# Rows of a weight tile padded from 642 to 648 columns, and one small copy moved from VectorE to ScalarE

## The chip, the cores and the metric

One core of one Trainium2 chip. The metric is the device time of one execution in microseconds (us).

## The reference

```python
x = A_x                                           # [1, 2048, 640] bf16
g = sigmoid((x * gate_w).sum(-1, keepdims=True))  # gate_w: 640
a = linear_attention(x, wqkv, w_phi, wo)          # 32 heads of 20, softmax feature maps
b = (silu(x @ w_gate) * (x @ w_up)) @ w_down      # 1728 wide
return g * a + (1 - g) * b
```

## The kernel before

The whole kernel is one static order of work. The change concerns its first microseconds and one tile, `wvg`, which holds the v part of `wqkv` and, as one more column, `gate_w`. A v projection of 128 tokens is ten matmuls into two PSUM banks: five rows `c` of the tile, each in two halves of 320 and 321 columns. The 321st column of the second half is the gate's sum.

```python
wvg = sb("wvg", [P, 5, D + 2], BF16)              # D = 640: a row is 642 columns, 1284 bytes

def v_pairs(t, pr):                               # ten matmuls for token tile t
    return [(bank(2 * pr + hb, 0, 320 + hb), xT[:, t, c, :],
             wvg[:, c, 320 * hb:640 + hb - 320 * (1 - hb)], c == 0, c == 4, False)
            for c in range(5) for hb in range(2)]

def xpose(t):                                     # "X": TensorE transposes an x tile, VectorE copies it out
    ...
def gcol():                                       # "G": gate_w, five rows of 128, becomes five columns
    pr = next_pair()
    o = bankbf(2 * pr, 8)[:, 0:5]
    transposes([(o, gwr[0:5, :])], 5)
    copy("dve", wvg[:, :, D:D + 1], o.unsqueeze(2))

def load_phi():                                   # "h": w_phi, issued by ScalarE once w3 has landed
    tr._wait("act", dict([wv_evs[3]]))
    dma("act", wph[:, :, :], ...)

LOADS = """x0 w0 x1 g w1 x2 w2 x3 w3 w4 f0 h k0 ..."""       # w0 to w4: rows of wvg; cut
ORDER = """H0 ... H12 X0 G X1 U0.0 U1.0 U0.1 X2 U1.1 U2.0 ...
... U0.4 U1.4 U2.4 V3 Y F0.1 M1 ...  K0 K1 ..."""            # cut
```

`H` are warm-up matmuls, `Ut.c` are the two matmuls of row `c` of v tile `t` (the first three tiles are done by rows, as their data land), `V` is a v tile in one go, `F` a piece of the feed-forward part, `M` premultiplies the k weights with blocks of w_phi that `Y` makes, `K` is a k projection. A helper puts a semaphore wait ahead of each instruction for what it reads and overwrites. Every engine does its instructions in this order.

The softmax here doesn't subtract the row's maximum and nothing guards it: scores larger than these inputs give would overflow.

## Time and profile before

| | kernel before |
|---|---|
| time, median of 3 | 288.74 us (288.39 to 288.85) |
| profiled span | 287.0 us |
| TensorE busy | 284.1 us, 99% |
| VectorE, ScalarE, GpSimd busy | 57%, 53%, 56% |

The prediction below shows the lines of the profile. A weight load (PEld) comes just ahead of its matmul (PE), and the idle time in brackets says what it waited for. And a matmul's end in the profile is modelled: a v matmul shows as 300 ns long, but the next one starts 136 ns later. What a matmul costs in a stream is the distance from its start to the next start.

### The profile page before, as it was taken

The numbers are of one execution on the slowest core, as the hardware profiler recorded it, in microseconds if no ns is written. First come the engines' busy times: TensorE is split into PE (matmuls) and PEld (weight loads), VectorE is DVE, ScalarE is ACT, GpSimd is POOL, SyncE is SP. The second block draws the span as 40 slices with busy tenths as digits, with TensorE's granted clock in tenths as the row PEclk, the third lists the DMA queues.
The fourth block names the chain that finished last, engine by engine and source line by source line (L and its number), as shares of the span: only waits on it lengthen the run. The fifth ranks groups of instructions, "written<-read, shape, count | busy, mean of one in ns | idle before, by whom it ended". The sixth has DMA issues, their size and how long they took to land.

```text
span 287.0 us, 4972 instructions
## 1 busy us (share of the span) xinstructions
PE 284.1 (99%) x1979; PEld 174.5 (61%) x1979; DVE 163.3 (57%) x243; ACT 152.4 (53%) x256; POOL 159.8 (56%) x125
## 2 busy tenths in 40 slices
PE   8999999999999999999999999999999999999997
PEld 6667777575644545557775556675554446666776
DVE  2337748576569978689991465970317899100000
ACT  0767778576775465683535753225676552234112
POOL 8286999879446789836543438350754558501000
PEclk9999999999999999999999999999999999999999
DMA  7977697000010598202383002061020006210101
GB/s 234 192 113 127 113 279 279 3 1 2 0 50 0 123 290 162 50 2 50 66 157 69 6 1 50 2 149 43 2 50 0 3 1 123 53 46 0 49 23 48
DMA packets 48944, 21.62 MB, mean 75 GB/s; under 512 B 39384, under 2 KB 48792, under 8 KB 48920
## 3 DMA queue, kind: packets, MB, share of 16 engines
q1 hardware_dynamic: 47400, 20.43, 31.5%
q10 hardware_dynamic: 1520, 0.87, 1.0%
q8 instruction: 16, 0.26, 0.4%
q14 instruction: 8, 0.07, 0.1%
HBM read 9.29 MB, written 2.62 MB: 42 GB/s over the span
## 4 chain that ended last, share of the span: by engine, by line
PE 99%; DVE 0%; issue 0%
PE ps L296 97%; PE ps L478 1%; PE ps L308 0%; DVE xT L320 0%; DVE osb L737 0%; DVE wvg L320 0%
## 5 line engine op out<-in xcount | busy, mean ns | idle before, releaser
L324 POOL TENSOR_TENSOR hT<-hT,us 128x512 bf16<-128x512 bf16 (+1 forms) x56 | 65.0, 1174 | 65.1 <-DVE hT L328 47.5
L328 DVE SCALAR_TENSOR_TENSOR hT<-hT,ps 128x512 bf16<-128x512 bf16 (+1 forms) x56 | 37.4, 683 | 66.8 <-ACT hT L314 53.0
L296 PE MATMUL ps<-xT,wg 128*128 128x512 bf16 x260 | 64.6, 379 | 0.0
L296 PE MATMUL ps<-xT,wu 128*128 128x512 bf16 x260 | 64.6, 379 | 0.0
L296 PE MATMUL ps<-wd,hT 128*128 128x320 bf16 (+2 forms) x462 | 63.9, 295 | 0.0
L324 POOL TENSOR_TENSOR ph<-eq,qc 128x1320 bf16<-128x1320 bf16 x16 | 42.4, 2647 | 25.6 <-DVE qc L638 20.8
L296 PEld LDWEIGHTS ps<-wd,hT 128*128 128x128 bf16 x462 | 44.5, 98 | 17.5 <-issue 0.2
L296 PE MATMUL ps<-wqk,xT 128*128 128x320 bf16 x320 | 47.7, 299 | 0.0
L314 ACT ACTIVATE hT<-ps 128x512 bf16<-128x512 f32 (+2 forms) x64 | 36.4, 569 | 16.8 <-PE ps L296 16.5
L296 PEld LDWEIGHTS ps<-xT,wu 128*128 128x128 bf16 x260 | 25.5, 98 | 30.6
L314 ACT ACTIVATE us<-ps 128x512 bf16<-128x512 f32 (+1 forms) x56 | 33.5, 598 | 18.5 <-PE ps L296 17.3
L314 ACT ACTIVATE osb<-ps,omg 128x640 bf16<-128x640 f32 (+2 forms) x17 | 12.9, 758 | 55.4 <-PE ps L296 55.4
L296 PEld LDWEIGHTS ps<-xT,wg 128*128 128x128 bf16 x260 | 25.1, 98 | 27.8 <-ACT osb L314 0.8
L324 POOL TENSOR_TENSOR ekr<-ekr,krec 128x1280 bf16<-128x1280 bf16 x16 | 37.4, 2358 | 5.8 <-DVE krec L338 5.8
L296 PEld LDWEIGHTS ps<-wqk,xT 128*128 128x128 bf16 x320 | 30.5, 98 | 13.1 <-issue 0.4
L314 ACT ACTIVATE eq<-ps 128x640 bf16<-128x640 f32 x32 | 22.4, 704 | 20.9 <-POOL ph L324 10.8
L335 DVE TENSOR_REDUCE ksum<-ekr 128x64 f32<-128x1280 bf16 x16 | 23.5, 1471 | 11.7 <-ACT ekr L314 11.7
L314 ACT ACTIVATE ekr<-ps 128x640 bf16<-128x640 f32 x32 | 22.3, 704 | 8.7 <-PE ps L296 8.2
L335 DVE TENSOR_REDUCE qz<-eq 128x64 f32<-128x1280 bf16 x16 | 23.6, 1478 | 2.6 <-ACT eq L314 2.6
L296 PE MATMUL ps<-wog,oT 128*128 128x320 bf16 (+2 forms) x165 | 24.7, 294 | 0.0
L296 PE MATMUL ps<-wvg,xT 128*128 128x320 bf16 (+1 forms) x160 | 24.1, 299 | 0.1
L335 DVE TENSOR_REDUCE qw<-ez 128x64 f32<-128x1280 bf16 x16 | 23.6, 1477 | 0.0
(73 smaller groups left out, 188.6 us busy)
## 6 DMA issues: line engine op xcount, KB each, us to landing
out_dram<-osb SPq DMA_DIRECT2D x15, 160.0 KB, 2.0
wd<-in_B_w_down_dram SPq DMA_DIRECT2D x1, 2080.0 KB, 9.2
wg<-in_B_w_gate_dram SPq DMA_DIRECT2D x1, 1040.0 KB, 10.0
wu<-in_B_w_up_dram SPq DMA_DIRECT2D x1, 1040.0 KB, 12.2
wg<-in_B_w_gate_dram SPq DMA_DIRECT2D x1, 800.0 KB, 6.1
wu<-in_B_w_up_dram SPq DMA_DIRECT2D x1, 800.0 KB, 7.7
wog<-in_A_wo_dram SPq DMA_DIRECT2D x2, 375.0 KB, 7.1
xs<-in_A_x_dram ACTq DMA_DIRECT2D x3, 160.0 KB, 4.2
```

Of the source, the lines that this page charges most:

```text
L296: last = pe.matmul(o, lhsT=l, rhs=r, start=st, stop=sp_, skip_group_check=sk)
L314: return run("act", lambda: act.activation(o, i, func, scale=scale), rd, [o])
L324: return run(e, lambda: eo.tensor_tensor(o, a, b, op), [a, b], [o])
L328: return run("dve", lambda: dve.scalar_tensor_tensor(out=o, in0=a, scalar=s, in1=b, op0=op0, op1=op1), rd, [o])
L335: return run("dve", lambda: dve.tensor_reduce(o, i, AX.X, ALU.add), [i], [o])
L478: last = pe.matmul(bank(2 * pr, 0, P), lhsT=c, rhs=c, start=True, stop=True)
```

## The change

The copy of the gate column goes to an engine that has nothing to do at that time. The w_phi load, at which ScalarE would otherwise stand first, goes behind it. The rows of the tile grow from 1284 to 1296 bytes.

```diff
-x0 w0 x1 g w1 x2 w2 x3 w3 w4 f0 h k0 k1 t4 ...
+x0 w0 x1 g w1 x2 w2 x3 w3 w4 f0 k0 k1 t4 ...
...
-H0 ... H12 X0 G X1 U0.0 U1.0 U0.1 X2 ...
+H0 ... H12 X0 G h X1 U0.0 U1.0 U0.1 X2 ...
...
-    wvg = sb("wvg", [P, 5, D + 2], BF16)
+    wvg = sb("wvg", [P, 5, D + 8], BF16)
...
-        copy("dve", wvg[:, :, D:D + 1], o.unsqueeze(2))
+        copy("act", wvg[:, :, D:D + 1], o.unsqueeze(2))
```

More of the change, by code (lines that the diff above doesn't have):

```diff
@@ L33 @@
 LOADS = """
-x0 w0 x1 g w1 x2 w2 x3 w3 w4 f0 h k0 k1 t4 k2 k3 k4 t5 t6 t7 t8 t9 t10 t11 t12 t13 t14 t15 q0 q1 q2 q3
+x0 w0 x1 g w1 x2 w2 x3 w3 w4 f0 k0 k1 t4 k2 k3 k4 t5 t6 t7 t8 t9 t10 t11 t12 t13 t14 t15 q0 q1 q2 q3
 q4 f1 f2
@@ L38 @@
 ORDER = """
-H0 H1 H2 H3 H4 H5 H6 H7 H8 H9 H10 H11 H12 X0 G X1 U0.0 U1.0 U0.1 X2 U1.1 U2.0 U0.2 U1.2 U2.1
+H0 H1 H2 H3 H4 H5 H6 H7 H8 H9 H10 H11 H12 X0 G h X1 U0.0 U1.0 U0.1 X2 U1.1 U2.0 U0.2 U1.2 U2.1
 X3 U2.2 U0.3 U1.3 U2.3 U0.4 U1.4 U2.4 V3 Y F0.1 M1 i3 M0 F0.0 M2 V4 M3 M4 K0 K1 I S0 V6 V5 S1 P0
```

## The prediction

> **What bounds the kernel now.** I read the page first (busy shares, then the chain that ended last), then the chain in order of time, then the timeline of the first 14 us, where everything that the change touches lies, and a table of stretches.
>
> From the page: the shares of busy time, and the chain that ended last by engine and by line.
>
> ```profile
> PE 284.1 (99%) x1979; PEld 174.5 (61%) x1979; DVE 163.3 (57%) x243; ACT 152.4 (53%) x256; POOL 159.8 (56%) x125
> ...
> PE 99%; DVE 0%; issue 0%
> PE ps L296 97%; PE ps L478 1%; PE ps L308 0%; DVE xT L320 0%; DVE osb L737 0%; DVE wvg L320 0%
> ```
>
> TensorE is the bound. No other engine is busy over 57%, and the chain is TensorE for 99% of the span. The last entry, the gate column's copy by VectorE, is the only thing of this change that stands on the chain. Its size is in the chain in order of time (start us, us, what):
>
> ```profile
> 3.77 0.72 PE ps L308 x5
> 4.50 0.02 issue
> 4.52 0.42 DVE xT L320
> 4.94 0.10 DVE wvg L320
> 5.04 0.05 issue
> 5.09 1.00 PE ps L296 x6
> 6.08 0.32 PE ps L308 x5
> ...
> 77.51 207.57 PE ps L296 x1275
> ```
>
> So VectorE copies the first x tile out of PSUM, copies the gate column behind it, and only then does TensorE start on the v projection, at 5.09. From there the chain is TensorE to the end. How much TensorE idles there is in the table of stretches (length, then busy us and count of each engine, granted clock, DMA share, GB/s):
>
> ```profile
> 3.70:5.10 1.40, 1.29 (x13) 0.84 (x13) 0.81 (x5) 0.00 (x0) 1.34 (x4) 1.00 1.00 325
> 5.10:6.00 0.90, 0.90 (x7) 0.54 (x8) 0.37 (x2) 0.00 (x0) 0.84 (x2) 1.00 1.04 358
> 100.00:285.00 185.00, 185.00 (x1169) 110.29 (x1166) 100.09 (x149) 86.96 (x139) 86.17 (x56) 1.00 0.26 59
> ```
>
> TensorE is idle for 1.40 - 1.29 = 0.11 us before the v projection, and not at all later as busy time counts it. Busy time hides short stalls, since the ends of matmuls are modelled, so I take the stalls from the weight loads in the timeline (start us, us, engine, what, idle time before it and what ended it):
>
> ```profile
> 4.52 0.42 DVE L320 COPY xT<-ps 128x512 bf16<-128x512 bf16 x1 [0.20 <-PE ps L308]
> ...
> 4.86 0.17 DVE L320 COPY wvg<-ps 128x5 bf16<-128x5 bf16 x1
> ...
> 5.08 0.66 PEld L296 LDWEIGHTS ps<-wvg,xT 128*128 128x128 bf16 x6 [0.28 <-DVE wvg L320]
> ...
> 5.95 0.28 PEld L308 LDWEIGHTS ps<-ident,xs 128*128 128x128 bf16 x5 [0.20 <-DMA xs<-in_A_x_dram]
> ...
> 7.30 0.40 ACTq L350 DMA_DIRECT2D wph<-in_A_w_phi_dram  x1
> ...
> 7.79 1.28 ACT L314 ACT_TABLE_LOAD   x1 [7.79 <-DMA wvg<-in_A_wqkv_dram]
> ...
> 9.46 0.71 ACT L314 ACTIVATE v1r<-ps 128x640 bf16<-128x640 f32 x1 [0.39 <-PE ps L296]
> ```
>
> Two stalls follow each other. Weight loads wait 0.28 us for the gate copy, run six matmuls, and then wait 0.20 us for the DMA of the third x tile (x2), whose completion the trace dates to 5.905. **The second one decides the case.** ScalarE in this time has nothing to do: its first instruction is the table load at 7.79, after the w_phi issue.
>
> **What the Trainium skill says.** "ScalarE: Activation LUTs", section "What ACT_TABLE_LOAD costs", gives about 1283 ns for the load, the same for every set, and 186 ns + 0.833 ns per element for an ACTIVATE with immediate scale and bias. The trace agrees on the first (1.28 us, 1283 ns). For 5 elements the second gives an estimate of 190 ns; the nearest in the trace, the 128x1 copy to svec, takes 165 to 224 ns. "SBUF — State Buffer", section "Operand start alignment", asks only that an operand start at a multiple of its element size, and says that this is about legality and that nothing was timed. "DMA: Bandwidth & Descriptors", section "How a descriptor splits into AXI transactions", has a descriptor pay extra beats when it doesn't start on 256 bytes; rows of 1296 bytes don't start there any more than rows of 1284. The trace shows no cost of the odd start: the 1280-byte packets of its DMA records take on average 55.1 ns for w3 and w4, which start 3 and 4 rows of 1284 bytes into the tile, and 55.0 ns for x1, whose rows start on 32 bytes.
>
> **The change part by part.**
>
> Padding: 642 to 648 columns, so each of the five rows starts 12 bytes further on, and the tile grows by 60 bytes. Tiles in this layout start on multiples of 32 bytes, so what follows moves by 64. No load gets larger: each still writes 1280 bytes a row. By the packets above the DMA gains nothing. Nor do the matmuls: those that read wvg take a mean of 299 ns, as do those of 320 columns that read wqk, whose rows are 1280 bytes. Worth: 0.
>
> VectorE loses one copy of 171 ns. It starts at 4.86 because the 0.42 us xT copy was ahead of it, not because its input was late: TensorE's gate transpose starts at 4.41 and ends at 4.60 (0.18 us). The next xT copy can start some 0.07 us earlier (4.93 to 4.86).
>
> ScalarE gets that copy. Its table load moves too, since it comes just before the first ACTIVATE. ScalarE's last issue ahead of it starts at 2.69 and takes 0.45 us, so the load would run from about 3.24 to 4.52 (in the kernel before it starts 0.09 us after the issue ahead of it). That is 0.08 us before the transpose ends. The copy would start at about 4.63 (0.04 us after its matmul, as the v1r copy at 9.465 after a matmul that ends at 9.429) and end at 4.63 + 0.19 = 4.82, against 5.03 now.
>
> So the first v matmul may start at 4.82 + 0.05 = about 4.88 instead of 5.09: **0.2 us gained at that place**, of which at most 0.11 us is idle time in the busy rows.
>
> What becomes of it: the six matmuls (U0.0, U1.0, U0.1) then end their issue 0.2 us earlier, and the transposes of x2 come next in TensorE's order. They can't start before x2 lands at 5.905. They start at 5.95 as before, and the stall of 0.20 us becomes about 0.4 us. From there everything stands as it did. Sum: -0.2 us at the first stall, +0.2 us at the second, **0.0 us** at the end.
>
> The w_phi load moves behind the copy in ScalarE's order, but it waits for w3, which lands at 7.285, and issues at 7.30. The copy is done 2.4 us before that. So w_phi is neither earlier nor later. ScalarE is free of the 1.28 us load at 7.79, but its next instruction waited 0.39 us for TensorE anyway.
>
> **The rivals.**
>
> A: the gain isn't absorbed. x2's landing would have to come earlier with the copy, for which nothing speaks: its DMA is issued at 2.21 and shares the queues with the same loads, at a DMA share of 1.04 in that stretch. Even then there is a further stop: the first premultiply needs the block weights, which GpSimd finishes at 12.95 (11.46 + 1.49) and whose first weight load is at 13.13, so less than 0.2 us would pass. Best outcome: 288.5.
>
> B: ScalarE becomes the wait. If the table load were held until the transpose is done, the copy would end near 4.63 + 1.28 + 0.19 = 6.10, and the v projection would start at 6.15, later by 1.06 us; nothing later gives that back while TensorE has no slack. The time would be 289.8, still within 2%. Against it: the load at 7.79 didn't wait for TensorE, while the ACTIVATE behind it did.
>
> C: padding speeds up the loads, so that x2 and w3 land earlier and w_phi with them. Even a twentieth off four tiles of 160 KB at 358 GB/s is an estimate of 0.09 us, and the packet times speak against it. 288.6 at best.
>
> **Range and chances.** The middle is the time before, 288.74, rounded to 288.7. The three runs before span 288.39 to 288.85, and a different chip or day may add as much again: 288.2 to 289.2. To leave 2%, 5.8 us would have to come or go, five times the largest rival and more than everything that TensorE does before 6 us. Chances: within 2% 0.98, the rest split evenly.
>
> **What would show it.** Right: the gate copy is on ScalarE, starting at about 4.6, behind a table load from about 3.2; the first weight load of the v projection is at 4.85 to 5.0; the weight load of the x2 transposes is still at about 5.95, with 0.3 to 0.45 us of idle time before it that the x DMA ended; w_phi issues at about 7.3; the first weight load on wbd stays near 13.13; the span is 287.0 within 0.3. Wrong on absorption: x2's transposes start with the v projection's shift and the span falls by 0.2. Wrong on ScalarE: the table load starts after 4.6 and the v projection after 6. Any change of a whole microsecond would mean that moving the tiles by 64 bytes, or the order of waits, does something that the trace before doesn't show.

## The result, and the profile after

| | before | after |
|---|---|---|
| time, median of 6 | 288.74 us (288.13 to 288.97) | 288.49 us (287.81 to 288.96) |
| profiled span | 287.0 us | 286.6 us |

The ratio is 0.9992, with a 95% interval of 0.9975 to 1.0009. A ratio here is the mean time of one kernel's fast runs over that of the other's of the same rounds, so not quite the ratio of the medians. The time is the same within 2%, and a ratio of 1, no change at all, lies in the interval.

The page of the changed kernel, shares of busy time and the chain by line:

```profile
PE 283.8 (99%) x1979; PEld 174.7 (61%) x1979; DVE 163.3 (57%) x242; ACT 152.5 (53%) x257; POOL 159.7 (56%) x125
...
PE ps L296 97%; PE ps L478 1%; PE ps L308 1%; DVE osb L737 0%
```

One instruction has moved from VectorE to ScalarE, and the gate copy is off the chain. The chain in order of time, changed kernel:

```profile
3.77 1.36 PE ps L308 x11
5.13 0.82 PE ps L296 x6
5.95 0.28 PE ps L308 x5
...
77.11 207.58 PE ps L296 x1275
```

TensorE now goes from the warm-up to the end with no other engine in between. The timeline of the changed kernel at the places that the prediction named:

```profile
3.18 1.28 ACT L314 ACT_TABLE_LOAD   x1 [3.18 <-issue]
...
4.61 0.19 ACT L314 ACTIVATE wvg<-ps 128x5 bf16<-128x5 bf16 x1
4.92 0.70 PEld L296 LDWEIGHTS ps<-wvg,xT 128*128 128x128 bf16 x6
...
5.65 0.40 PEld L308 LDWEIGHTS ps<-ident,xs 128*128 128x128 bf16 x5
...
7.27 0.41 ACTq L350 DMA_DIRECT2D wph<-in_A_w_phi_dram  x1
```

Table load, copy, first v weight load and w_phi issue stand within 0.1 us of where the prediction had them. But the weight load for the x2 transposes, which was to stay at 5.95 behind its DMA, is at 5.65 with no wait. In this execution x2 landed at 5.515, not at 5.905.

That explains a shift of some 0.17 us at that point. The last matmul, however, starts 0.40 us earlier (284.47 against 284.86). To find the rest I laid the starts of the 1979 matmuls of both traces side by side. The shift is 165 ns at the x2 transposes and grows to 397 ns at the last matmul, by some 15 ns with each v tile; 226 of the 232 ns of growth fall on v matmuls. (Other tiles were moved by 64 bytes too, but the matmuls that read them keep their pace.) Twenty v matmuls in a row, and twenty k matmuls of the same size behind them, first in the kernel before:

```profile
21.18 2.92 PE L296 MATMUL ps<-wvg,xT 128*128 128x320 bf16 x20
23.93 2.88 PE L296 MATMUL ps<-wqk,xT 128*128 128x320 bf16 x20
```

and the same in the changed kernel:

```profile
20.95 2.89 PE L296 MATMUL ps<-wvg,xT 128*128 128x320 bf16 x20
23.67 2.88 PE L296 MATMUL ps<-wqk,xT 128*128 128x320 bf16 x20
```

The k matmuls keep their 2.88 us and the v matmuls fall from 2.92 to 2.89. By rows, the mean distance from start to start is this (from the twelve v tiles behind the first feed-forward matmul, each done in one go: 24 matmuls for each row, 12 for each half):

| row of wvg | 0 | 1 | 2 | 3 | 4 |
|---|---|---|---|---|---|
| before: start, bytes past a multiple of 16 | 0 | 4 | 8 | 12 | 0 |
| before: ns, halves of 320 / 321 | 135.5 / 136.5 | 139.8 / 139.2 | 138.2 / 139.2 | 138.5 / 139.2 | 135.0 / 136.0 |
| after: start, bytes past a multiple of 16 | 0 | 0 | 0 | 0 | 0 |
| after: ns, halves of 320 / 321 | 135.6 / 136.4 | 135.8 / 136.6 | 135.9 / 136.8 | 135.8 / 136.6 | 135.9 / 136.8 |

(The second half of a row starts 640 bytes on, which is a multiple of 16.) So the theory that I took to the chip had two parts. **Rows:** a matmul whose right, moving operand starts off a 16-byte boundary takes some 3 ns more in the stream; 96 of the 160 v matmuls did so. **Head** (the first microseconds, up to the first feed-forward matmul)**:** the copy on ScalarE brings the first v matmul forward by 0.1 us, and whether that survives depends on when x2 lands. The rival: everything is chance of the DMA and of TensorE's clock in single executions.

### The profile page after: what moved, and what is told of

Read it like the earlier page. It is cut to its first block, busy times and chain, and to the rows that moved or that the text cites. A ratio compares the mean times of both kernels' runs of the same rounds, so it can differ in the third digit from the quotient of the medians.

```text
span 286.6 us, 4972 instructions
## 1 busy us (share of the span) xinstructions
PE 283.8 (99%) x1979; PEld 174.7 (61%) x1979; DVE 163.3 (57%) x242; ACT 152.5 (53%) x257; POOL 159.7 (56%) x125
## 4 chain that ended last, share of the span: by engine, by line
PE 99%; DVE 0%; issue 0%
PE ps L296 97%; PE ps L478 1%; PE ps L308 1%; DVE osb L737 0%
```

## The experiments

There were twelve runs of eight kernels, all with correct results. Those of one submission ran on one chip beside the kernel before, whose times are quoted with them. A table at the end of this section has the start times.

### e1_after_again: the changed kernel once more

No edit.

> The changed kernel once more. Theory: two small gains add up, about 0.25 us from the padded rows (each v matmul whose right operand starts off a 16-byte boundary starts its successor some 3 ns later; 96 of 160 do before, none after) and 0.0 to 0.2 us at the head, so 288.3 to 288.5 against 288.7 and a ratio of 0.9985 to 0.9995; twenty v matmuls in a row take 2.89 us, not 2.92. Rival (all of it is noise of the x tile's landing and of the clock's warm-up): a ratio of 1.000 within 0.0005, and twenty v matmuls take 2.92 us as in the kernel before.

Measured: 288.40 us (288.04 to 289.80, one of six at 289.80) against 288.52, ratio 1.0007 (0.9989 to 1.0024). The time can't tell. The trace does: ten v matmuls of a tile take 1361.8 ns from start to start, 1362.0 in the first profile of the changed kernel and 1377.3 before.

### e2_pad_only and e6_pad_only_again: only the rows

```diff
-    wvg = sb("wvg", [P, 5, D + 2], BF16)
+    wvg = sb("wvg", [P, 5, D + 8], BF16)
```

> Only the rows are padded; VectorE still copies the gate column and the w_phi load keeps its place. Theory: all 160 v matmuls keep the pace of 136 to 137 ns from start to start, so twenty in a row take 2.89 us and the time falls by about 0.25 us, ratio 0.9991; the v projection still starts at about 5.09, after VectorE's copy. Rival (padding does nothing): 2.92 us for twenty, ratio 1.000.

> Padding alone, a second time. Theory: from the first k matmul to the last matmul TensorE takes 266.24 us again (266.41 with rows of 642 columns, in every run so far), twenty v matmuls 2.89 us; the ratio is near 0.9992 and within 0.0015 of it. Rival (the 0.17 us are chance): 266.3 to 266.5.

Measured: 288.14 us against 288.52, ratio 0.9997 (0.9982 to 1.0011), and 288.33 against 288.39, ratio 0.9995 (0.9982 to 1.0009). The line of twenty v matmuls in e2_pad_only:

```profile
21.23 2.89 PE L296 MATMUL ps<-wvg,xT 128*128 128x320 bf16 x20
```

From the first k matmul to the last matmul TensorE takes 266.236 us in both, 266.405 in the kernel before. This stretch holds eleven of the sixteen v tiles, thus 66 of the 96 matmuls that started off a 16-byte boundary: 0.169 us, 2.6 ns each. The pace of the v matmuls is the padding's doing.

### e3_copy_only and e5_copy_only_again: only the copy and the place of the w_phi load

```diff
-        copy("dve", wvg[:, :, D:D + 1], o.unsqueeze(2))
+        copy("act", wvg[:, :, D:D + 1], o.unsqueeze(2))
```

with `h` moved as in the change, and rows of 642 columns.

> Only ScalarE's copy and the later place of the w_phi load; rows stay at 642 columns. Theory: twenty v matmuls take 2.92 us as before, the v projection starts at 4.9 to 5.0 instead of 5.09, and 0.0 to 0.2 us of it reaches the end, ratio 0.9993 to 1.000. Rival that the pace of the v matmuls comes from the copy's engine and not from the rows: 2.89 us.

> ScalarE's copy alone, a second time: the first time its profile had TensorE at half pace until 6.6 us (six v matmuls took 1.72 us, 1.00 in the kernel before), and it came out 0.17% slower. Theory: that is where TensorE's clock happened to rise in that execution, not the copy. So this time six v matmuls take about 1.0 us in the profile, the first v matmul follows the first x transpose by 1.20 to 1.22 us (1.32 with VectorE's copy), and the ratio is 0.9993 to 1.000 within its interval. Rival: the copy or the early table load itself delays the clock's rise, so the profile again shows six v matmuls in 1.5 us or more and the ratio is near 1.0017 again.

Measured: 288.88 us against 288.52, ratio 1.0017 (1.0003 to 1.0031), then 288.61 against 288.39, ratio 1.0006 (0.9992 to 1.0019). Twenty v matmuls take 2.92 us again, and the stretch from the first k matmul is 266.406 and 266.402 us, so the copy's engine has nothing to do with the pace. The head of the first profile:

```profile
5.07 1.72 PE L296 MATMUL ps<-wvg,xT 128*128 128x320 bf16 x6
```

Six matmuls took 1.72 us, 1.00 in the kernel before: they started 267 ns apart instead of 136. TensorE ran at half pace until about 6.6 us. (This trace has no clock record at all and its table of stretches reads 1.00, so the half pace is seen in the starts alone.) The second profile has 0.98 us for the six, so the copy doesn't bring this about each time. It shows the other half of the prediction's argument instead:

```profile
5.88 0.28 PEld L308 LDWEIGHTS ps<-ident,xs 128*128 128x128 bf16 x5 [0.32 <-DMA xs<-in_A_x_dram]
```

Here x2 landed at 5.833, and the early v projection merely waited longer, as predicted. The prediction's second stop is seen too: w3 landed late, at 7.589, w_phi was issued at 7.61, and the first premultiply came 2.28 us after the first gate matmul, not 2.16 as in the other profiles. The first time's slower result is not explained by this, since all of its five runs count. Pooled, ten runs with the copy alone have a mean of 288.76 us, 39 runs of the kernel before 288.51, ten runs with the padding alone 288.31 and eighteen of the changed kernel 288.47 (over different chips; the standard error of each mean is 0.06 to 0.12 us). Whether the copy on ScalarE gains 0.1 us in the time, or loses something, is not settled by these: it stays **open**.

### e4_misalign_all: odd rows for the other weights too

```diff
-    wqk = sb("wqk", [P, 2, 5, D], BF16)
+    wqk = sb("wqk", [P, 2, 5, D + 2], BF16)
-    wog = sb("wog", [P, 5, D], BF16)
-    wd = sb("wd", [P, 14, D], BF16)
+    wog = sb("wog", [P, 5, D + 2], BF16)
+    wd = sb("wd", [P, 14, D + 2], BF16)
```

on the kernel before; reads and loads of these tiles take the first 640 columns.

> The kernel before with 642 columns a row for the q, k, output and down weights too, whose rows of 640 columns all start on 16 bytes now. 653 more matmuls then have a right operand that starts 4, 8 or 12 bytes off (96 of q, 128 of k, 99 of the output weights, 330 of the down weights). Theory: 653 times 3.2 ns is 2.1 us, so about 290.8 us and a ratio of 1.007; twenty k or q matmuls take 2.92 us or more, not 2.88. Rival (the start of the right operand costs nothing, and the quicker v matmuls have another cause): 288.7 us, ratio 1.000, 2.88 us.

Measured: 289.76 us against 288.52, ratio 1.0051 (1.0038 to 1.0065), clear of noise. The k matmuls, which took 2.88 us:

```profile
23.95 2.91 PE L296 MATMUL ps<-wqk,xT 128*128 128x320 bf16 x20
```

The direction is the theory's, the size is not: the stretch from the first k matmul grew by 1.20 us, which over 653 matmuls is 1.8 ns each, not 3.2. In the down weights, rows that start off a 16-byte boundary have 137.6 to 138.7 ns, but rows 4, 8 and 12, which start on one, fell from 135.7 to 135.9 down to 135.0 or 135.1. The 3.2 ns had compared the two kinds within one kernel; a row on the boundary behind one off it gets some of the cost back. So part of the 3.2 ns was never a loss to the stream.

### e8_row_pitch_dose: which starts cost

```diff
-    wqk = sb("wqk", [P, 2, 5, D], BF16)
+    wqk = sb("wqk", [P, 2, 5, D + 1], BF16)
-    wog = sb("wog", [P, 5, D], BF16)
-    wd = sb("wd", [P, 14, D], BF16)
+    wog = sb("wog", [P, 5, D + 8], BF16)
+    wd = sb("wd", [P, 14, D + 4], BF16)
```

on the changed kernel.

> The changed kernel with rows of 641 columns for q and k (starts 0, 2, 4 ... 14 bytes past a multiple of 16), 644 for the down weights (starts 0 or 8 past it) and 648 for the output weights (multiples of 16, every other one not of 32). Theory: only starts that are not multiples of 16 cost, about 2.5 to 3 ns each from start to start: q and k mean 138 instead of 136 ns, down weights 137 to 137.5 instead of 135.8, output weights as before at 137.6. 256 of q and k and 231 of the down weights are off, so +1.0 to +1.4 us on the changed kernel, ratio to before 1.003 to 1.004. Rival A, starts off 4 bytes alone cost: nothing for the down weights. Rival B, starts off 32 bytes cost: the output weights rise by 1 ns or more.

Measured: 289.35 us against 288.39, ratio 1.0029 (1.0015 to 1.0044). The stretch from the first k matmul grew by 0.80 us over the changed kernel's, less than the 1.0 to 1.4 expected, 1.65 ns for each of the 487. That is a mean of two kinds: 2.4 to 2.7 ns for q and k, where four rows of five are off, and 1.0 ns for the down weights, where every second row is off and the rows between take 135.0 ns instead of 135.8. By rows, from the trace:

| tile and row | start, bytes past a multiple of 16 | ns from start to start |
|---|---|---|
| down weights, even rows 2 to 12 | 0 | 135.0 |
| down weights, odd rows 1 to 11 | 8 | 137.5 to 137.8 |
| k weights, row 3 | 0 | 135.0 |
| k weights, rows 1, 2, 4 | 12, 14, 2 | 138.3, 139.2, 138.6 |
| output weights, rows 1, 3 (off 32 bytes, on 16) | 0 | 135.0, 135.8 |
| output weights, row 2 (on 32 bytes) | 0 | 135.8 |

Every start off 16 bytes costs, 2 and 8 and 14 too; off 32 but on 16 costs nothing. Both rivals of this run fall. The k and v lines of the run have changed places:

```profile
21.39 2.89 PE L296 MATMUL ps<-wvg,xT 128*128 128x320 bf16 x20
24.11 2.92 PE L296 MATMUL ps<-wqk,xT 128*128 128x320 bf16 x20
```

### e7_held_table and e12_held_table_again: the copy made late

```diff
-        transposes([(o, gwr[0:5, :])], 5)
+        _, v = transposes([(o, gwr[0:5, :])], 5)
+        act.wait_ge(tr.sem["pe"], v)
```

on the changed kernel, so that ScalarE's table load waits for the transpose.

> The changed kernel with ScalarE's table load held until the gate column's transpose is done (a second wait ahead of it). Theory: the table load then lies on the path, 1.28 us from about 4.65, the copy ends near 6.15 and the first v matmul starts at about 6.2 instead of 5.0. Nothing later gives it back, so the time is 1.1 to 1.2 us longer than the changed kernel's: 289.6, ratio to before 1.003 to 1.004. Rival (the head has slack: the third x tile's landing, or the block weights, end the wait anyway): under 0.4 us of it reaches the end, ratio under 1.001.

> The kernel with the held table load again: its six executions were three at 289.2 and three at 290.6 to 291.0, and the profile had fallen on a 289.2, in which the pace after the wait was full. Theory: in the other mode TensorE's clock drops or rises late around the 1.4 us of idle time, and a profile of it shows six v matmuls in 1.7 us or more and matmuls at 267 ns for about 3 us in all. Rival: the slower mode has the same head and loses its 1.5 us elsewhere. If the profile falls on 289.2 again, this stays open.

The timeline of the first of the two:

```profile
4.72 1.28 ACT L314 ACT_TABLE_LOAD   x1 [4.72 <-PE ps L308]
6.01 0.19 ACT L314 ACTIVATE wvg<-ps 128x5 bf16<-128x5 bf16 x1
...
6.35 0.98 PE L296 MATMUL ps<-wvg,xT 128*128 128x320 bf16 x6 [1.26 <-ACT wvg L314]
```

This is the prediction's rival B, made on purpose. The first v matmul starts 1.38 us later than in the changed kernel's first profile (6.350 against 4.968), and so does the last one (285.85 against 284.47): the head has no slack beyond what x2 may take. The times are in two groups, two at 289.2 and four at 290.6 to 291.0 (the expectation of the repeat miscounts them as three and three; median 290.68, ratio 1.0070, 1.0049 to 1.0090). The profile fell on the first group both times, and the two runs of the repeat, on another chip, were 288.90 and 288.96. What the other 1.5 us are stays **open**; the next run suggests TensorE's clock.

### e9_copy_w_phi_first: the copy without the move of the w_phi load

The changed kernel with `h` back in the list of loads.

> The changed kernel with the w_phi load back at its old place, ahead of the gate copy in ScalarE's order. Theory: ScalarE then stands at the w_phi load until w3 lands (7.2 to 7.9 us in the profiles so far), issues it for 0.4 us, loads its table for 1.28 us and only then copies the gate column: first v matmul at 9.2 to 9.9 instead of 5.0, and all of the 4.3 us or more reaches the end. TensorE is idle for over 4 us, so its clock may fall back and the first matmuls after it run at half pace (267 ns from start to start instead of 136), which adds up to 1.7 us. 292.6 to 294.5, ratio 1.014 to 1.021. Rival (there is slack behind the head): under 1.010.

Measured: 294.40 us against 288.53, ratio 1.0202 (1.0181 to 1.0223), clear of noise. Its timeline, with ScalarE issuing w_phi only when w3 has landed, then its table load, then the copy:

```profile
7.13 0.41 ACTq L350 DMA_DIRECT2D wph<-in_A_w_phi_dram  x1
7.57 1.28 ACT L314 ACT_TABLE_LOAD   x1 [7.57 <-DMA wvg<-in_A_wqkv_dram]
8.86 0.19 ACT L314 ACTIVATE wvg<-ps 128x5 bf16<-128x5 bf16 x1
...
9.20 1.76 PE L296 MATMUL ps<-wvg,xT 128*128 128x320 bf16 x6 [4.19 <-ACT wvg L314]
```

and the table of stretches (length, busy us of the engines, then granted clock, DMA share, GB/s):

```profile
3.70:9.30 5.60, 1.39 (x13) 0.96 (x13) 1.15 (x4) 1.48 (x2) 3.35 (x7) 0.88 1.11 319
9.30:12.70 3.40, 3.40 (x17) 2.12 (x17) 0.65 (x2) 0.00 (x0) 1.28 (x3) 0.50 1.00 174
```

The wait costs twice. TensorE starts the v projection 4.2 us late, and its clock has fallen to a half meanwhile: the clock records of the trace have it full from 4.51 to 7.92, half to 14.75, then full. The last matmul is 6.9 us later than in the changed kernel's first profile, so the half pace adds 2.7 us to the wait, not the 1.7 expected. The move of the w_phi load thus belongs to the copy: without it, the kernel is 2% slower.

### e10_x2_one_later: the x2 transposes behind one more pair

```diff
-... U0.0 U1.0 U0.1 X2 U1.1 U2.0 ...
+... U0.0 U1.0 U0.1 U1.1 X2 U2.0 ...
```

on the changed kernel: an attempt to beat both.

> The changed kernel with the transposes of the third x tile one place later, behind a further pair of v matmuls that needs nothing new. Theory: in 4 of 10 profiles those transposes waited for their DMA, by 0.05 to 0.5 us; a pair of matmuls is 0.27 us, so in such executions up to 0.27 us less, in the others nothing: 0.1 us on average, ratio to before 0.9985 to 0.9995, and no wait for the x DMA at that place in the profile unless it lands after 6.1. Rival (the order of those two makes a new wait, the copy of the third tile being later for the matmul behind it): the distance from the first v matmul to the first gate matmul of the feed-forward grows from 6.00 us, where no DMA is late, to 6.2 or more.

Measured: 288.65 us against 288.53, ratio 0.9997 (0.9977 to 1.0018). A miss, and the rival of this run is seen:

```profile
7.54 0.93 PEld L296 LDWEIGHTS ps<-wvg,xT 128*128 128x128 bf16 x8 [0.27 <-DVE xT L320]
```

The pair that was moved had hidden VectorE's copy of x2; now `U2.0` waits 0.27 us for it (0.16 before). From the first v matmul to the first gate matmul 7.04 us passed, 6.01 in the changed kernel's first profile. Only 0.26 us of that is the new wait. The other 0.75 us come from TensorE's clock, which in this profile rose only during the sixth v matmul: the first five starts are each followed by the next after 266 to 271 ns, the sixth after 234.

### e11_after_third: the changed kernel beside it

> The changed kernel a third time, beside the one with the transposes later. Theory: from the first k matmul to the last 266.24 us as in its two other profiles; the head varies with the landing of the x tiles and with where the clock rises, by some 0.5 us; ratio 0.9992 within 0.0015. Rival (the change is worth nothing): ratio 1.000 or more.

Measured: 288.56 us against 288.53, ratio 0.9994 (0.9977 to 1.0012), and 266.237 us from the first k matmul to the last one.

### The starts of single matmuls

From the traces: starts in us of the first x transpose, the first v matmul and the first x2 transpose, then the length of two stretches, from there to the first gate matmul of the feed-forward part and from the first k matmul to the last matmul.

| run | rows | copy | first x | first v | x2 | x2 to gate | first k to last |
|---|---|---|---|---|---|---|---|
| before | 642 | VectorE | 3.768 | 5.087 | 5.950 | 5.240 | 266.405 |
| e3_copy_only | 642 | ScalarE | 3.805 | 5.074 | 6.633 | 5.229 | 266.406 |
| e5_copy_only_again | 642 | ScalarE | 3.702 | 4.913 | 5.880 | 5.237 | 266.402 |
| e2_pad_only | 648 | VectorE | 3.923 | 5.243 | 6.070 | 5.191 | 266.236 |
| e6_pad_only_again | 648 | VectorE | 3.899 | 4.959 | 6.304 | 5.200 | 266.236 |
| after | 648 | ScalarE | 3.746 | 4.968 | 5.785 | 5.191 | 266.237 |
| e1_after_again | 648 | ScalarE | 3.919 | 5.121 | 5.935 | 5.191 | 266.240 |
| e11_after_third | 648 | ScalarE | 3.811 | 5.076 | 5.931 | 5.191 | 266.237 |
| e7_held_table | 648 | ScalarE | 3.805 | 6.350 | 7.165 | 5.190 | 266.239 |

The two right columns follow the rows alone, to 4 ns in the last one. The middle ones move by 0.2 us and more with the landing of the x tiles and with the moment at which TensorE's clock rises, in every kernel.

## Why the prediction was right or wrong

**The time** was right: 288.7 foretold, 288.49 measured, no change beyond noise. That proves little for the parts: the range of 288.2 to 289.2 is wider than all that the prediction had wrong, and by the traces its sum of 0.0 us should have been -0.2 to -0.3.

**TensorE as the bound, ScalarE idle, no harm from the early table load:** right. Rival B needed a held table load, and e7_held_table shows what that would have cost.

**Padding, "Worth: 0":** this is the step that failed. DMA packets gave no reason to expect anything, and that part no run contradicts. But for the matmuls the prediction compared mean durations, 299 and 299 ns, whose ends are modelled; they read 299 ns after the change too, so they don't show this cost. The distances from start to start in the trace of before, 139 and 136 ns, had it in plain sight. (Nor does each row start 12 bytes further on, as it says: row `c` starts 12 times `c` further on, which takes the starts of rows 1 to 3 from 4, 8 and 12 bytes past a multiple of 16 to none.) Its size: 0.169 us after the first k matmul, 0.015 us for the v tile ahead of that (7.269 to 7.254 from the first gate to the first k matmul), and 0.03 to 0.05 us in the first three tiles (5.229 to 5.240 against 5.190 to 5.200): together about **-0.22 us**. The Trainium skill states the unit: "SBUF — State Buffer", section "Specifications (TRN2)", gives 16-byte cachelines, with a penalty for each crossing to a new line. I had read only the same page's section on the legal start of an operand. The size of the line is the boundary found here. But the number of lines touched doesn't explain the cost. Half a row of 320 columns is 640 bytes, 40 lines, and 41 when it starts inside one; a half of 321 columns touches 41 from either start, and yet took 139.2 ns off the boundary and 136.4 to 136.8 on it. How the cost comes about stays open.

**The gain at the first v matmul:** its place was right, its size too large. Measured from the first x transpose to the first v matmul, 1.32 us with VectorE's copy became 1.20 to 1.27 with ScalarE's, a gain of 0.05 to 0.12 instead of 0.2. The copy itself ended at 4.80, as foretold (4.82). The term that was mis-sized is the hand-off behind it: the prediction took the 0.05 us between VectorE's copy and the v weight load for ScalarE's too, but in all ten profiles with ScalarE's copy the weight load starts 0.11 us after the copy's end, against 0.05 in all four with VectorE's. In some profiles up to 0.07 us more pass, because TensorE is still transposing x1, at half pace until its clock has risen. (e6_pad_only_again, where the clock rose before the first transpose, has 1.06 with VectorE.)

**Its absorption at x2:** right as a mechanism, wrong as a certainty. x2 landed at 5.905 in the one profile that I had, and between 5.2 and 6.3 in the others. In e5_copy_only_again the gain was absorbed as foretold; in the three profiles of the changed kernel x2 was there in time. The prediction's own sign of being wrong on absorption came true in the first of them: the x2 transposes moved with the v projection, and the span was 286.6, outside its 287.0 within 0.3. One profile gives one sample of a landing time, and I took it for a constant. "Everything stands as it did" behind it should have been "in this execution".

**The w_phi load and the premultiply:** right. It issued at 7.27 against 7.30, and the first weight load on the blocks is at 12.95 against 13.13, with the rest of the head.

The sum of the parts, -0.22 us from the rows and at most -0.12 from the copy, is 0.1% of the time. The pooled means resolve neither part: padding alone is 0.20 us below before, but the changed kernel, with the same rows, is 0.04 below, and each difference has a standard error of about 0.12. What the rows are worth is shown by the starts in the traces, not by the times.

## What to carry to other kernels

Let every row of a tile that TensorE streams start on a multiple of 16 bytes: here each bf16 matmul of 320 columns with another start cost a net 1.0 to 2.7 ns of 136, by how many of its neighbours were off as well. Its mean duration in the profile doesn't show this; the distance from start to start does. When work moves to another engine, look at what that engine stands waiting for in its own order: this copy of 0.19 us would have cost 6 us behind a load. And read a DMA's landing time in one profile as one draw: this one spread over a microsecond.

## What the Trainium skill lacked or had wrong

- "SBUF — State Buffer", section "Specifications (TRN2)", has the 16-byte lines but not what they mean for a matmul's moving operand; no page that I found says it. Here: bf16, 128x320, starts of 2, 4, 8, 12 or 14 bytes past a line take 137.2 to 139.8 ns from start to start, starts on a line 135.0 to 136.8; net of what the neighbours get back, 1.0 to 2.7 ns for each matmul with such a start. Its section "Operand start alignment" says that its runs timed nothing, so a reader may take any legal start for free, as the prediction did.
- "TensorE: Matmul & The Clock Gate", section "Part 1: The HAM clock gate (the "warmup" mystery)", has a free-running window of 3413 ns and a clock that falls to a half after idle time. e9_copy_w_phi_first agrees (full for 3.41 us, half for 6.83 us). What it doesn't say is how little work in a window is too little: the window at whose end the clock fell, 4.51 to 7.92 us, held the five transposes of x1 (4.56 to 4.79), while after the wait of 1.26 us in e7_held_table's profile the matmuls went on at full pace.
